# A clustered attention's slot in another order: scores between the two groups of transposes, the exponential between their evictions, the row maximum between the low parts

## The chip, the cores and the metric

One core of a Trainium2 chip. The time of a run is device microseconds from launch to end; the kernel before took 782.77 us in the median of three runs (782.29, 782.77 and 786.18).

## The reference

Attention over 2 batches, 8 heads, 768 positions of 64 elements: each query and key is assigned to the nearest of 16 centroids of its head, and a query attends only to keys of its own cluster. Two MLP layers follow on the 1536 rows of 512 elements.

```python
q_assign = argmax(q_n @ c_n.T); k_assign = argmax(k_n @ c_n.T)
scores = where(q_assign[..., :, None] == k_assign[..., None, :], (q @ k.T) / 8, -1e9)
attn = softmax(scores)                 # rows of 768
x = (attn @ v) laid out as [1536, 512]
x = softplus(x @ w_in1) @ w_out1       # 512 -> 2048 -> 512
h = x @ w_in2
out = (h * clip(h + 3, 0, 6) / 6) @ w_out2
```

## The kernel before

Everything is computed in pairs of a high and a low part: a value is rounded to fp32r (the high part), and the remainder is the low part; products of the parts are summed in PSUM.

The attention runs over 8 pairs of heads (2 batches x 4 pairs). A pair has 12 slots: 2 heads x 6 tiles of 128 query rows. So there are 96 slots. In each slot one tile of queries goes through these steps, named by the functions that issue them:

- `scores(t)`, line 403: four matmuls (512 and 256 columns, two terms each) into a score tile `s` of PSUM. There are two such tiles.
- `row_max(t)`, line 414: VectorE reduces the 768 columns to the negated maximum `nm`.
- `expo(t)`, line 419: ScalarE takes the exponential into the probability tile `pr`, with the row sums read from the accumulator.
- `flip(t, g)`, line 429, for g = 0 and 1: three transposes of `pr` into a PSUM tile `t` (two tiles in all, so a group uses the tile of the same group a slot earlier), then the eviction: ScalarE copies `t` to the high part `pth` (line 442), and VectorE subtracts to make the low part `ptl` (line 443). A tile `t` is free when its low part is done.
- `weigh(h, c)`, line 445: four matmuls of 384 columns of an earlier half head (three slots) with the values.
- `gather(h, step)`, line 458: after every third slot the finished half head is taken out of PSUM by two ScalarE copies of 64 partitions, one into `rest` and one into `main`; GpSimd adds them later. The product of head 0 of a pair has its main part on partitions 0 to 63 and head 1's on 64 to 127.

The order of the work is written by hand (`tc.manual_schedule`). Each engine takes its instructions strictly in the order of the code, and waits for semaphores where tiles demand it. The loop over slots (line 817) has seven places, 0 to 6, between its steps; `at(slot, place, function, ...)` puts the other work there: loading and splitting the next pair's q and k, its cluster masks (`p_sims` to `p_mask`, lines 293 to 368: similarities, their maximum, one-hot, transposed back), their assembly by DMA into the operands `Q` and `K` (`assemble`, `assemble_mask`), the sums' reciprocals (`total`, `tot_flip`), and weights of the first MLP layer. In the text o is the first of the 12 slots ahead of a pair in which its masks are made.

The MLPs follow: 96 steps of 24 matmuls of 512 columns, from some 256 us to the end.

## Time and profile before

| what | value |
|---|---|
| median of three runs | 782.77 us |
| profiled execution | 782.03 us, its span 780.2 us |
| TensorE busy | 768.9 us, 99% of the span |
| VectorE, ScalarE, GpSimd busy | 456.3, 416.9 and 151.0 us |
| granted TensorE clock | 0.999 |
| slots 0 to 95 | from 17.8 to some 250 us |

A busy time is the time in which an engine's records cover the clock. TensorE's matmuls overlap one another, so that a busy engine may still be held up; the weight loads (PEld) of a matmul stand in a row of their own, and waits of TensorE mostly show there. The waits and the timeline name the instruction that waited and, after the arrow, whose end released it.

### The profile page before, as it was taken

To read this page: it belongs to the slowest core of one execution; us is meant where nothing else is said; L and a number is where in the kernel's file an instruction comes from. 1 tells how busy PE (TensorE), PEld (TensorE's weight loads), DVE (VectorE), ACT (ScalarE), POOL (GpSimd) and SP (SyncE) were. 2 spreads that over 40 slices of the span, in tenths; PEclk is the share of its full clock that TensorE was granted. 3 is DMA by queue.
4 is the path that set the end of the run, shared out by engine and by line. 5 is a ranking of instruction groups with operands and counts; after the bars stand their busy time and mean duration, and the time that the engine had idled before them with its cause. 6 is when DMAs were issued, how large, how long until landed. Compare 5 with 4: busy or idle time off the path is not lost.

```text
span 780.2 us, 10575 instructions
## 1 busy us (share of the span) xinstructions
PE 768.9 (99%) x3841; PEld 642.1 (82%) x3841; DVE 456.3 (58%) x788; ACT 416.9 (53%) x830; POOL 151.0 (19%) x222
## 2 busy tenths in 40 slices
PE   7999999999999999999999999999999999999998
PEld 6788888888888788888888888888888888888886
DVE  6988888888988999721111276879752322232222
ACT  6899988988998766522122254545532222222221
POOL 3666756856434000000000000000000000000000
PEclk9999999999999999999999999999999999999999
DMA  7647667557381760000000365640000100010001
GB/s 190 186 128 178 145 158 188 136 157 172 87 249 56 267 240 0 1 1 0 1 1 27 110 207 176 210 135 0 1 1 0 55 1 0 1 55 0 1 1 54
DMA packets 39124, 69.75 MB, mean 89 GB/s; under 512 B 4480, under 2 KB 24096, under 8 KB 39072
## 3 DMA queue, kind: packets, MB, share of 16 engines
q1 hardware_dynamic: 39072, 69.08, 30.9%
q8 instruction: 30, 0.49, 0.3%
q14 instruction: 22, 0.18, 0.1%
HBM read 46.30 MB, written 3.19 MB: 63 GB/s over the span
## 4 chain that ended last, share of the span: by engine, by line
PE 88%; DVE 5%; ACT 3%; issue 1%; POOL 1%; DMA 1%; POOLq 0%; ACTq 0%; DVEq 0%; SPq 0%
PE h L169 32%; PE y L895 17%; PE y L893 16%; PE t L438 7%; PE s L408 6%; PE pv L453 6%; PE psm L308 2%; DVE ptl L443 1%; DVE nm L416 1%; ACT pth L442 1%; ACT pr L424 1%; DMA rsb<-row 0%; DMA row<-rT 0%; PE warm L245 0%; ACT xs L468 0%
## 5 line engine op out<-in xcount | busy, mean ns | idle before, releaser
L169 PE MATMUL h<-xhi,pi 128*128 128x512 f32 x768 | 238.5, 392 | 0.6 <-DVE pi L144 0.5
L169 PEld LDWEIGHTS h<-xhi,pi 128*128 128x128 f32 x768 | 143.8, 188 | 32.3 <-DVE pi L144 1.0
L874 DVE TENSOR_TENSOR glo<-g,ghi 128x512 fp32r<-128x512 f32 x96 | 66.3, 691 | 146.2 <-ACT ghi L861 117.4
L169 PE MATMUL h<-xlo,pi 128*128 128x512 f32 x384 | 149.9, 390 | 0.0
L895 PE MATMUL y<-po,ghi 128*128 128x512 f32 x384 | 118.9, 391 | 0.0
L893 PE MATMUL y<-ghi,po 128*128 128x512 f32 x384 | 118.8, 391 | 0.0
L443 DVE TENSOR_TENSOR ptl<-t,pth 128x384 fp32r<-128x384 f32 x192 | 97.8, 550 | 28.0 <-ACT pth L442 27.8
L867 DVE SCALAR_TENSOR_TENSOR g<-u,h 128x512 f32<-128x512 f32 x48 | 33.0, 688 | 127.2 <-ACT u L863 127.1
L863 ACT ACTIVATE u<-h,half 128x512 f32<-128x512 f32 x48 | 33.0, 687 | 128.3 <-PE h L169 128.0
L416 DVE TENSOR_REDUCE nm<-s 128x1 f32<-128x768 f32 x96 | 90.7, 945 | 3.7 <-PE s L408 3.7
L442 ACT ACTIVATE pth<-t 128x384 fp32r<-128x384 f32 x192 | 85.7, 487 | 11.8 <-PE t L438 11.4
L408 PE MATMUL s<-K,Q 128*128 128x256 f32 (+1 forms) x384 | 89.9, 356 | 1.7 <-ACT pr L424 1.1
L438 PE MATMUL t<-ident,pr 128*128 128x128 f32 x576 | 88.3, 280 | 1.2 <-DVE ptl L443 0.7
L424 ACT ACTIVATE pr<-s,nm 128x768 f32<-128x768 f32 x96 | 86.5, 901 | 3.5 <-DVE nm L416 3.2
L860 ACT ACTIVATE g<-h 128x512 f32<-128x512 f32 x48 | 28.5, 595 | 110.8 <-PE h L169 110.8
L169 PEld LDWEIGHTS h<-xlo,pi 128*128 128x128 f32 x384 | 72.1, 188 | 15.7
L895 PEld LDWEIGHTS y<-po,ghi 128*128 128x128 f32 x384 | 72.1, 188 | 15.6
L893 PEld LDWEIGHTS y<-ghi,po 128*128 128x128 f32 x384 | 72.0, 188 | 15.6
L438 PEld LDWEIGHTS t<-ident,pr 128*128 128x128 f32 x576 | 64.0, 140 | 20.4 <-DVE ptl L443 15.4
L408 PEld LDWEIGHTS s<-K,Q 128*128 128x128 f32 x384 | 65.8, 189 | 11.5 <-ACT pr L424 2.3
L895 PE MATMUL y<-po,glo 128*128 128x512 f32 x192 | 75.1, 391 | 0.0
L893 PE MATMUL y<-glo,po 128*128 128x512 f32 x192 | 75.0, 391 | 0.0
(123 smaller groups left out, 937.9 us busy)
## 6 DMA issues: line engine op xcount, KB each, us to landing
ri<-in_moe_w_in SPq DMA_DIRECT2D x29, 512.0 KB, 4.6
ro<-in_moe_w_out SPq DMA_DIRECT2D x29, 512.0 KB, 4.8
K<-hik SPq DMA_DIRECT2D x31, 192.0 KB, 5.3
Q<-hiq SPq DMA_DIRECT2D x15, 384.0 KB, 4.1
Q<-loq SPq DMA_DIRECT2D x16, 192.0 KB, 5.6
v<-in_v SPq DMA_DIRECT2D x8, 384.0 KB, 6.6
rsb<-row SPq DMA_DIRECT2D x16, 192.0 KB, 3.8
out<-o SPq DMA_DIRECT2D x12, 256.0 KB, 3.5
```

The costliest lines, as they stand in the source:

```text
L169: nc.tensor.matmul(hs[n][:, :TB], w[:, c, :], x[c][:, cols], start=(c == 0 and i == 0), stop=(c == NC - 1 and i == 2))
L408: nc.tensor.matmul(ps[:, n0:n1], Q[i][:, u, j * P:(j + 1) * P], K[i][:, u, n0:n1], start=(u == 0), stop=(u == 1),)
L416: nc.vector.tensor_reduce(nm, st_s[t][:, :S], AX.X, ALU.max, negate=True)
L424: nc.scalar.activation(pr, st_s.pop(t)[:, :S], AF.Exp, bias=st_p[t], accum_out=sums_of[n][:, i, j:j + 1])
L438: nc.tensor.transpose(pt[:, c * P:(c + 1) * P], pr[:, kt * P:(kt + 1) * P], ident)
L442: last_flip[:] = [nc.scalar.activation(dh, src, AF.Copy)]
L443: nc.vector.tensor_tensor(dl, src, f32(dh), ALU.subtract)
L453: nc.tensor.matmul(st_v[h][:, :HALF], vs[:, kt, i, :], st_t[h][u][:, kt, :], start=(kt == 0 and u == 0), stop=(kt == NJ - 1 and u == 1),)
L863: nc.scalar.activation(t["u"], t["h"], AF.Relu, bias=half, scale=1.0 / 6.0)
L874: nc.vector.tensor_tensor(t["glo"], t["g"], f32(t["ghi"]), ALU.subtract)
L893: nc.tensor.matmul(y[:, :TB], w[:, e, :], x, **fl)
L895: nc.tensor.matmul(y, x[:, e * P:(e + 1) * P], w.rearrange("p c e -> p (c e)"), **fl)
```

## The change

In a slot the transposes of group 0 now come first, then the scores of the slot three ahead, then the transposes of group 1, then the weighing. On ScalarE the copy of group 0 comes first, then the exponential of the slot two ahead (it was one ahead, so three `pr` buffers), then the copy of group 1. On VectorE the row maximum of the slot three ahead (it was two) stands between the two low parts.

TensorE in two slots of the second pair's time (`t` transposes, `s` scores, `pv` weighing), before:

```order
L438 MATMUL t<-ident,pr 128x128 x6
L408 MATMUL s<-K_155,Q_153 128x512 x2
L408 MATMUL s<-K_155,Q_153 128x256 x2
L453 MATMUL pv<-pth,vs 128x384
L453 MATMUL pv<-ptl,vs 128x384
L453 MATMUL pv<-pth,vs 128x384
L453 MATMUL pv<-ptl,vs 128x384
L483 MATMUL pb<-ident,rs 12x128
L438 MATMUL t<-ident,pr 128x128 x6
```

and now:

```order
L438 MATMUL t<-ident,pr 128x128 x3
L408 MATMUL s<-K_156,Q_154 128x512 x2
L408 MATMUL s<-K_156,Q_154 128x256 x2
L438 MATMUL t<-ident,pr 128x128 x3
L453 MATMUL pv<-pth,vs 128x384
L453 MATMUL pv<-ptl,vs 128x384
L453 MATMUL pv<-pth,vs 128x384
L453 MATMUL pv<-ptl,vs 128x384
L438 MATMUL t<-ident,pr 128x128 x3
L408 MATMUL s<-K_157,Q_155 128x512 x2
L408 MATMUL s<-K_157,Q_155 128x256 x2
L438 MATMUL t<-ident,pr 128x128 x3
```

The block of six transposes is cut into three and three, with the scores between them.

ScalarE in the slots after a head's gathering (`pth` copies, `pr` exponential, `xs` gathering, `sT` similarities), before:

```order
L424 ACTIVATE pr,sums<-s,nm 128x768
L466 ACTIVATE xs_1004<-pv 64x384
L468 ACTIVATE xs_1003<-pv 64x384
L442 ACTIVATE pth<-t 128x3x128 x2
L314 ACTIVATE sT<-psm,c_r 128x384
L424 ACTIVATE pr,sums<-s,nm 128x768
L442 ACTIVATE pth<-t 128x3x128 x2
L424 ACTIVATE pr,sums<-s,nm 128x768
```

and now:

```order
L442 ACTIVATE pth<-t 128x3x128
L468 ACTIVATE xs_1107<-pv 128x384
L442 ACTIVATE pth<-t 128x3x128
L424 ACTIVATE pr,sums<-s,nm 128x768
L442 ACTIVATE pth<-t 128x3x128 x2
L424 ACTIVATE pr,sums<-s,nm 128x768
L442 ACTIVATE pth<-t 128x3x128 x2
L424 ACTIVATE pr,sums<-s,nm 128x768
```

The copies no longer stand in pairs; a copy of group 1 is followed by the next slot's copy of group 0 (x2). The gathering shown is one of head 0: a single copy of 128 partitions where there were two of 64.

VectorE, numbers kept (`ptl` low parts, `nm` row maximum), before:

```order
L416 TENSOR_REDUCE nm_1105<-s_1093 128x1
L443 TENSOR_TENSOR ptl_1112<-t_1113,pth_1111 128x3x128
L443 TENSOR_TENSOR ptl_1112<-t_1119,pth_1111 128x3x128
L416 TENSOR_REDUCE nm_1144<-s_1126 128x1
L443 TENSOR_TENSOR ptl_1112<-t_1146,pth_1111 128x3x128
L443 TENSOR_TENSOR ptl_1112<-t_1152,pth_1111 128x3x128
```

and now:

```order
L443 TENSOR_TENSOR ptl_1008<-t_1096,pth_1007 128x3x128
L443 TENSOR_TENSOR ptl_1112<-t_1113,pth_1111 128x3x128
L416 TENSOR_REDUCE nm_1126<-s_1121 128x1
L443 TENSOR_TENSOR ptl_1112<-t_1128,pth_1111 128x3x128
L443 TENSOR_TENSOR ptl_1112<-t_1145,pth_1111 128x3x128
L416 TENSOR_REDUCE nm_1160<-s_1155 128x1
L443 TENSOR_TENSOR ptl_1112<-t_1162,pth_1111 128x3x128
```

Each maximum stands between the low parts of one slot.

Further: for head 0 of a pair `gather` copies all 128 partitions at once into `main`, and a DMA moves the other half into `rest` (16 copies less, 16 DMAs more). The steps of the mask making are put at other places of their slots, mostly after the slot's transposes. The tile `eq` is bf16 and the one-hot is made in place. The centroids lie in the tile of v, with the part that is needed longer copied by GpSimd to `cT`; the zeroing of `oh` goes from VectorE to GpSimd, and some small tiles share a buffer.

```diff
--- before
+++ after
@@ -176,7 +176,7 @@
             ld = st_ld.enter_context(tc.tile_pool(name="ld", bufs=1, side="right"))
             tp = st_ld.enter_context(tc.tile_pool(name="tp", bufs=2, side="right"))
             qk = pool("qk", 1)
-            pp = pool("pp", 2)
+            pp = pool("pp", 3)
             vsp = pool("vs", 2)
             ptp = pool("ptp", 2)
             xs_p = pool("xs", 1)
@@ -213,8 +213,8 @@
                 raws[n, "v"] = t
 
 
-            cent = cb.tile([P, NPAIR * (C + D)], F32, name="cent")
-            cT = cent[:, :NPAIR * C].rearrange("p (n c) -> p n c", c=C)
+            cent = ld.tile([P, S], F32, tag="v", name="cent")[:, :NPAIR * (C + D)]
+            cT = cb.tile([P, NPAIR, C], F32, name="cT")
             c_sb = cent[:, NPAIR * C:].rearrange("p (n d) -> p n d", d=D)
             load_qk(0, "q", lambda: nc.sync.dma_start(cent, centroids))
             load_qk(0, "k")
@@ -332,7 +332,7 @@
             def p_equal(n):
                 d = prep[n]
                 sv, mx = d["pb"], d["mx"]
-                eq = sm.tile(full, F32, tag="eq", name="eq", bufs=1)
+                eq = sm.tile(full, BF16, tag="eq", name="eq", bufs=1)
                 nc.vector.tensor_tensor(eq, sv, mx.unsqueeze(2).to_broadcast(full), ALU.is_equal)
                 d["eq"] = eq
 
@@ -349,8 +349,8 @@
 
             def p_first(n):
                 d = prep[n]
-                oh = sm.tile(full, BF16, tag="oh", name="oh", bufs=1)
-                nc.vector.tensor_tensor(oh, d["eq"], d["mx2"].unsqueeze(2).to_broadcast(full), ALU.is_equal)
+                oh = d["eq"]
+                nc.vector.tensor_tensor(oh, oh, d["mx2"].unsqueeze(2).to_broadcast(full), ALU.is_equal)
                 d["oh"] = oh
 
             def p_onehot(n):
@@ -462,7 +462,12 @@
                     xs_of[n, hf] = [xs_p.tile([P, HALF], F32, tag=f"xs{u}", name=f"xs{u}", bufs=(4, 2)[u]) for u in range(2)]
                 pv = st_v[h]
                 main, rest = xs_of[n, hf]
-                if step == 0:
+                if i == 0:
+
+                    if step == 0:
+                        nc.scalar.activation(main, pv[:, :HALF], AF.Copy)
+                        nc.sync.dma_start(rest[a:a + D], main[z:z + D])
+                elif step == 0:
                     nc.scalar.activation(rest[a:a + D], pv[z:z + D, :HALF], AF.Copy)
                 elif step == 1:
                     nc.scalar.activation(main[a:a + D], pv[a:a + D, :HALF], AF.Copy)
@@ -484,7 +489,7 @@
                 sums_of[n] = pb
 
             def tot_out(n):
-                rT = sm.tile([2 * NJ, P], F32, tag="rT", name="rT", bufs=1)
+                rT = sm.tile([2 * NJ, P], F32, tag="sT", name="rT", bufs=1)
                 nc.scalar.activation(rT, sums_of[n][:2 * NJ, :P], AF.Copy)
                 row = dr.tile([2, S], F32, tag="row", name="row")
                 nc.sync.dma_start(row.rearrange("h (j t) -> (h j) t", t=P), rT)
@@ -548,14 +553,14 @@
                     at(o + 0, 4, p_sims_out, n)
                     at(o + 1, 1, p_back, n)
                     at(o + 1, 4, p_max, n)
-                    at(o + 2, 2, p_equal, n)
+                    at(o + 2, 4, p_equal, n)
                     at(o + 2, 4, p_rank, n)
-                    at(o + 4, 2, p_best, n)
-                    at(o + 5, 2, p_first, n)
-                    at(o + 6, 3, p_onehot, n)
-                    at(o + 7, 1, p_mask, n)
+                    at(o + 4, 4, p_best, n)
+                    at(o + 5, 4, p_first, n)
+                    at(o + 6, 4, p_onehot, n)
+                    at(o + 6, 6, p_mask, n)
                     at(o + 4, 1, assemble, n, 0)
-                    at(o + 7, 2, assemble_mask, n, 0)
+                    at(o + 7, 1, assemble_mask, n, 0)
                     at(o + 10, 5, assemble, n, 1)
                     at(o + 11, 4, assemble_mask, n, 1)
                     at(o + -3, 6, load_v, n)
@@ -584,8 +589,8 @@
                 o += 2 * SL
                 if n < NP - 1:
                     at(o + -2, 4, total, n)
-                    at(o + 3, 0, tot_flip, n)
-                    at(o + 3, 4, tot_out, n)
+                    at(o + 3, 4, tot_flip, n)
+                    at(o + 3, 6, tot_out, n)
                     at(o + 4, 4, tot_spread, n)
                     for hf in range(2):
                         if n < NP - 2:
@@ -693,7 +698,7 @@
             at(99, 3, lambda: convert_rest(*pieces0[5], engine=nc.vector))
 
 
-            c_sq = sm.tile([P, HALF], F32, tag="eq", name="c_sq", bufs=1)[:, :NPAIR * D].rearrange("p (n d) -> p n d", d=D)
+            c_sq = sm.tile([P, HALF], F32, tag="mk", name="c_sq", bufs=1)[:, :NPAIR * D].rearrange("p (n d) -> p n d", d=D)
             c_ss = cb.tile([P, NPAIR], F32, name="c_ss")
             c_n = cb.tile([P, NPAIR], F32, name="c_n")
             c_r = cb.tile([P, NPAIR], F32, name="c_r")
@@ -719,6 +724,7 @@
                     nc.tensor.transpose(warm[:, :P], ident, ident)
 
 
+            nc.gpsimd.tensor_copy(cT.rearrange("p n c -> p (n c)"), cent[:, :NPAIR * C])
             p_centroids(0)
             clear(1)
             p_split_hi(0, "q", 0)
@@ -750,8 +756,8 @@
             p_back(0)
             warm_up(14)
 
-            oh = sm.tile(full, BF16, tag="oh", name="oh", bufs=1)
-            nc.vector.memset(oh, 0.0)
+            oh = sm.tile(full, BF16, tag="sT", name="oh", bufs=1)
+            nc.gpsimd.memset(oh, 0.0)
             prep[0]["oh"] = oh
 
             def one_head(i, parts=range(5)):
@@ -816,26 +822,25 @@
             p_values(0, 1)
             for s in range(-3, NS + 7):
                 extras(s, 0)
-                if 2 <= s + 1 < NS:
-                    expo(s + 1)
+                if 0 <= s < NS:
+                    flip(s, 0)
                 extras(s, 1)
                 if 2 <= s + 2 < NS:
-                    row_max(s + 2)
+                    expo(s + 2)
                 extras(s, 2)
-                if 0 <= s < NS:
-                    flip(s, 0)
+                if 2 <= s + 3 < NS:
+                    scores(s + 3)
+                    row_max(s + 3)
                 extras(s, 3)
                 if 0 <= s < NS:
                     flip(s, 1)
                 extras(s, 4)
-                if 2 <= s + 3 < NS:
-                    scores(s + 3)
                 extras(s, 5)
                 h, c = s // JH - 1, s % JH
                 if 0 <= h < 4 * NP:
                     weigh(h, c)
                     if c == JH - 1:
-                        for step, where in enumerate((2, 2, 4)):
+                        for step, where in enumerate((0, 0, 4)):
                             at(s + 1, where, gather, h, step)
                 extras(s, 6)
             assert not extra, extra
```

## Rows read from the trace of the kernel before

**Rows 1.** The page's first part: busy us, share of the span, instructions of each engine
```profile
PE 768.9 (99%) x3841; PEld 642.1 (82%) x3841; DVE 456.3 (58%) x788; ACT 416.9 (53%) x830; POOL 151.0 (19%) x222
```

**Rows 2.** Windows: stretch, sum of length, busy us (instructions) by engine, clock, DMA
```profile
140.00:160.00 20.00, 19.99 (x129) 16.85 (x129) 17.93 (x31) 19.02 (x45) 17.16 (x24) 1.00 0.60 145
320.00:340.00 20.00, 20.00 (x90) 16.56 (x89) 6.95 (x12) 5.45 (x10) 0.00 (x0) 1.00 0.00 0
```

**Rows 3.** Waits from 34 to 230 us: who waited for whom, total us, times, longest
```profile
PEld t L438 <- DVE ptl L443: 13.1, 61, 0.5
...
PEld s L408 <- ACT pr L424: 0.9, 3, 0.5
```

**Rows 4.** Timeline of TensorE in a slot without waits: start, us, engine, line, count
```profile
231.66 0.82 PE L438 MATMUL t<-ident,pr 128*128 128x128 f32 x6
232.24 0.94 PE L408 MATMUL s<-K,Q 128*128 128x512 f32 x4
233.02 0.33 PE L453 MATMUL pv<-pth,vs 128*128 128x384 f32 x1
...
233.72 0.82 PE L438 MATMUL t<-ident,pr 128*128 128x128 f32 x6
```

**Rows 5.** Timeline of weight loads for transposes (PEld), two slots with waits
```profile
145.82 0.31 PEld L438 LDWEIGHTS t<-ident,pr 128*128 128x128 f32 x3 [0.17 <-DVE ptl L443]
146.29 0.31 PEld L438 LDWEIGHTS t<-ident,pr 128*128 128x128 f32 x3 [0.15 <-DVE ptl L443]
...
148.07 0.31 PEld L438 LDWEIGHTS t<-ident,pr 128*128 128x128 f32 x3
```

**Rows 6.** Timeline of ScalarE (ACT) in the same stretch
```profile
143.68 0.48 ACT L466 ACTIVATE xs<-pv 64x384 f32<-64x384 f32 x1
144.18 0.49 ACT L468 ACTIVATE xs<-pv 64x384 f32<-64x384 f32 x1
...
145.60 0.88 ACT L424 ACTIVATE pr<-s,nm 128x768 f32<-128x768 f32 x1
...
146.48 0.89 ACT L442 ACTIVATE pth<-t 128x384 fp32r<-128x384 f32 x2
147.26 0.90 ACT L424 ACTIVATE pr<-s,nm 128x768 f32<-128x768 f32 x1
```

**Rows 7.** Timeline of VectorE (DVE) in the same stretch
```profile
145.21 1.02 DVE L443 TENSOR_TENSOR ptl<-t,pth 128x384 fp32r<-128x384 f32 x2 [0.38 <-ACT pth L442]
146.15 0.95 DVE L416 TENSOR_REDUCE nm<-s 128x1 f32<-128x768 f32 x1
147.02 0.54 DVE L348 TENSOR_REDUCE mx<-eq 128x24 f32<-128x384 f32 x1
147.47 1.01 DVE L443 TENSOR_TENSOR ptl<-t,pth 128x384 fp32r<-128x384 f32 x2
```

**Rows 8.** Timeline: a slot's six transposes on TensorE
```profile
139.17 0.82 PE L438 MATMUL t<-ident,pr 128*128 128x128 f32 x6
```

**Rows 9.** Timeline of ScalarE: the eviction of rows 8
```profile
139.69 0.87 ACT L442 ACTIVATE pth<-t 128x384 fp32r<-128x384 f32 x2 [0.51 <-PE t L438]
```

**Rows 10.** Timeline of all engines in the first slots
```profile
12.31 0.36 DVE L775 TENSOR_TENSOR oh<-eq,mx 128x192 bf16<-128x192 f32 x1
...
18.37 1.98 POOL L282 TENSOR_TENSOR lok<-k,hik 128x384 fp32r<-128x384 f32 x2 [7.96 <-ACT hik L268]
19.47 1.10 DVE L775 TENSOR_TENSOR oh<-eq,mx 128x192 bf16<-128x192 f32 x1
...
21.00 0.67 ACT L367 ACTIVATE mk<-po,mbi,msc 128x384 fp32r<-128x384 bf16 x1 [0.36 <-PE po L361]
...
23.61 0.58 SPq L397 DMA_DIRECT2D Q<-mk  x1
...
26.19 0.94 PE L408 MATMUL s<-K,Q 128*128 128x512 f32 x4
```

**Rows 11.** The mask's transfers (line 397) over the whole run
```profile
DMA to landing us min/median/max: 1.8/2.0/5.0
```

## The prediction, made before the changed kernel ran

> **What bounds the kernel now.** I read the busy times first. TensorE is busy for 99% of the span [rows 1], so one might stop there. But its records overlap, and the windows say little more: 19.99 of 20 us in a stretch of the attention, 20.00 in one of the MLPs [rows 2]. In the attention ScalarE (19.02 of 20) and VectorE (17.93) are nearly full too [rows 2]; three engines hand each slot round in a ring, and each is held to its written order.
>
> So the waits come next. From 34 to 230 us, some seven pairs of heads (28 us each), the weight loads of the transposes waited 61 times and 13.1 us for a low part, that is, for VectorE to free a tile `t`; those of the scores waited 0.9 us for an exponential [rows 3]. These 14.0 us, 2.0 per pair, are what a better order can win there. The timeline confirms that they are lost time: a slot without waits takes 233.72 - 231.66 = 2.06 us (transposes 0.58, scores 0.78, weighing 0.70) [rows 4]; one with waits of 0.17 and 0.15 takes 148.07 - 145.82 = 2.25 [rows 5].
>
> The weight loads are busy for 16.85 us of 20 in the attention and 16.56 in the MLP stretch [rows 2]; in the latter matmul follows matmul without a wait, so a load share of 16.6 is a full TensorE. The Trainium skill (Perfetto Trace Analysis, Identifying the Most-Contended Engine) says that matmul busy time is no good measure of TensorE's headroom, and names the busy share of the weight loads instead. The first half the trace bears out; by the second the attention would have 16% to give, 31 us of these 196, and the time would be 752. By the waits it is 14. I take the waits.
>
> **The change part by part: the slot.** Durations: transposes to the start of their copy 139.69 - 139.17 = 0.52 [rows 8, 9]; a copy of 384 columns 0.49 [rows 6], and the next activation starts 0.39 after it (two copies, 147.26 - 146.48 = 0.78) [rows 6]; exponential with its sums 146.48 - 145.60 = 0.88 until the next starts [rows 6]; a low part 0.55 (two in 1.02, so the second starts 0.47 after the first), a row maximum 0.87 until the next starts [rows 7].
>
> The new slot, from the start of its first transposes at 0: scores at 0.29, transposes of group 1 at 1.07, weighing at 1.36, next slot at 2.06. ScalarE: copy 0 from 0.52, exponential from 0.91, copy 1 from 1.79 to 2.28, free at 2.18 for what can overlap; the next copy 0 can start at 2.58, so 0.40 is to spare. VectorE: low part 0 at 1.05, maximum at 1.52, low part 1 from 2.39 to 2.94, free at 2.86; next low part 0 at 3.11, so 0.25 is to spare. Group 1 of the next slot wants its tile `t` at 2.06 + 1.07 = 3.13: a slack of 0.19. A plain slot therefore runs without a wait.
>
> Gatherings and mask steps disturb it. The two copies of a gathering start 0.50 apart and end the ScalarE spare: 0.48 + 0.49 [rows 6], about 1.0 before copy 0. Now head 0 needs one such copy, 0.5: 0.40 is spare, so everything moves by 0.10, within the slack. Head 1 still needs 1.0: 0.60 late, 0.41 beyond the slack, and TensorE waits that long. Of head 1's two gatherings per pair one falls in slot o, whose six similarity matmuls of 384 columns (weighing's four take 0.70 [rows 4], so six take 1.05) give ScalarE more time than it needs. On VectorE each of the four mask steps of 0.45 (147.47 - 147.02) [rows 7] exceeds the spare by 0.20; they come in two neighbouring pairs of slots, and the second of each makes group 1 wait 0.2. Together 0.41 + 2 x 0.2 = 0.8 us per pair stay.
>
> The same reckoning for the old order: low part 1 ends at 2.05 and group 1 of the next slot wants its tile at 2.35; any gathering of 1.0 after the exponential costs 0.46, four times a pair, and the mask steps add 0.4: 2.2 against 2.0 measured (less for slot o). So it can be trusted to some 0.3 per pair. Gain: 14.0 - 7 x 0.8 = 8.4 us. Its ends: 14.0 when nothing stays, and 0 when all stays.
>
> **The other parts.** The 16 new DMAs stand in SP's queue at place 0 of a slot, waiting for a ScalarE copy that is issued just before; behind them come the mask's transfers, a slot (2.06 us) later. That slot hides them: 0; without it, the 0.58 of one issue [rows 10] on two slots of seven pairs, at most 8 us.
>
> The start. The first pair's second mask (`mk`, at 21.00) now stands behind the exponential of slot 3 (0.88), which waits for a maximum (0.87) that now follows the one-hot step on VectorE: 1.75 later. Its last transfer was issued at 23.61, transfers land 2.0 after issue [rows 11], so at 25.6, and the scores that need it started at 26.19 [rows 10]: 0.6 in hand. Cost 1.75 - 0.6 = 1.1 us; from 0 (if the steps before it speed up as well) to 2.6 (if nothing is in hand and a maximum more stands in front).
>
> GpSimd's copy of the centroids stands ahead of the first similarity matmuls. No row shows one of 64 columns; one of 384 takes 0.99 [rows 10]. Between 0 and 0.99; in proportion to the columns it is 0.16, and I take 0.2. The end: the last exponential comes a slot earlier, so the last slots, which have no scores, may shorten: 0 to 1, I take 0.3. The bf16 `eq` and the in-place one-hot: not shown; the one-hot step took 0.36 alone and 1.10 while GpSimd ran a subtraction [rows 10], so seven of them differ by -2 to +5 us in all if every one met or missed GpSimd; they stand behind low parts with 0.25 to spare, and I take 0. The zeroing on GpSimd has until that step's input is ready: 0. Waits of the MLPs do not change, since their stage starts earlier as a whole.
>
> Sum: 8.4 - 1.1 - 0.2 + 0.3 = 7.4 us off the profiled execution's 782.0, 774.6. The median of the runs stands 0.7 above that execution, so the forecast is 775.4 us.
>
> **The rivals.** (1) All waits go: 14.0 instead of 8.4, 769.8. For it: spare time on all engines, and ScalarE has 16 copies of 0.49 less. Against it: head 1's gathering is as long as before.
>
> (2) The wait only changes its place, and the time stays: 782. Group 1's copy now stands behind an exponential, and the slack is 0.19 in each slot. If the chain is 0.29 longer than I reckon, every plain slot waits 0.10, and 84 of them give back the 8.4. For it: a ring of three full engines [rows 2]. The copies no longer come in pairs; an exponential right behind a copy still starts 0.11 before that ends (147.26 against 146.48 + 0.89) [rows 6], so no overlap need be lost. The Trainium skill (ScalarE: Activation LUTs, What ACT_TABLE_LOAD costs) says that activations back to back overlap by about 93 ns, which these rows bear out. What the rule holds against the change is that a copy that has to wait for its transposes is not back to back: two of them lose an estimated 0.19 per slot by the page's figure, the whole slack. By it the time lies between the forecast and this rival; by the rows it is the forecast.
>
> (3) Slower: the copy behind the exponential makes every slot late. Low part 1 now ends a slot's chain: transposes, copy 0, exponential, copy 1, low part 1. From the point where it ends more than 0.19 late in a plain slot TensorE pays each further tenth in every one of 84 slots. With 0.36 late it is 84 x 0.17 = 14.3, and with the 5.6 that stay and the 1.0 at start and end 20.9 against the 14.0 of now: 789.7. For it: the copy of group 1 moved from 0.39 to 1.27 behind copy 0. Against it: VectorE's own order would hold low part 1 until 2.39 anyhow, 0.11 after copy 1 ends, so only a delay of both counts.
>
> **How the numbers follow.** The forecast (771.5 to 779) 0.54; rival 1 (below 771.5) 0.12; rival 2 (779 to 786) 0.21; rival 3 (above 786) 0.13. About 0.5%, 3.9 us, is what a measurement of this kernel can tell from no change: faster is below 778.9, slower above 786.7. Faster: 0.54 + 0.12, and a little less for the border, 0.65; same 0.22; slower 0.13. The range for 8 in 10 goes from 769, which leaves out some 0.05 of rival 1, to 785, which leaves out rival 3. The forecast's own range is 771.5 to 779.
>
> **What the changed kernel's profile would show.** The step on the slot is right if TensorE's waits for low parts fall from 13.1 us to about 5, those left being mostly of the second group and in slots with head 1's gathering, and if plain slots take 2.06. It is wrong if waits for a low part stand in nearly every slot (rival 2 or 3), or if none are left (rival 1). The gathering is right if 16 ScalarE copies of 128 partitions stand where 32 of 64 did. The start is right if the first scores of head 1 begin about 27.3. A wait of the scores for a mask transfer in later pairs, or of a copy for the exponential ahead of it with TensorE idle, would make the forecast wrong.

## The result and the profile after

The changed kernel takes 787.49 us in the median of ten runs, the kernel before 782.25 in ten beside them: a ratio of 1.0061, 95% interval 1.0048 to 1.0075. It is slower by 5.2 us, where 775.4 was forecast and 769 to 785 was the range. The profiled executions are 787.78 and 782.03 us long.

Where the 5.8 us of the two spans arose is read from four marks in the timelines: the first transposes of slots 0, 12 and 84, and the load of the activation table behind the attention's last eviction (lines 860 and 865). The table lists the experiments too; times in us, "first" is the first pair, slots 0 to 11, "end" goes from slot 84 to the table load, and "MLPs after" from there to the end of the span. A row's parts are of one profiled execution, its median is of all runs; e3's profiled execution (784.70) was the slowest of its twelve runs.

| kernel | first | slots 12 to 83 | end | MLPs after | median |
|---|---|---|---|---|---|
| before | 31.85 | 171.92 | 29.12 | 529.6 | 782.25 |
| changed | 32.40 | 172.97 | 33.26 | 529.6 | 787.49 |
| e3: old order, all other parts | 36.60 | 168.97 | 30.02 | 529.7 | 783.36 |
| e4: old order, merged gathering alone | 33.56 | 168.23 | 29.90 | 530.0 | 780.12 |
| e13: new order, two copies | 31.89 | 175.48 | 33.59 | 529.6 | 791.44 |
| e14: old order, repaired | 30.09 | 170.04 | 28.99 | 530.9 | 779.50 |

So 4.1 of the 5.8 us lie in the last twelve slots, 1.1 in the six middle pairs, which were to give 7 us, and 0.5 in the first pair.

The page's first part, for the changed kernel (before: [rows 1]), shows TensorE at 97% instead of 99%, and ScalarE 8 us shorter, as 16 copies of 128 partitions should make it:

```profile
PE 765.7 (97%) x3841; PEld 644.9 (82%) x3841; DVE 460.9 (59%) x787; ACT 408.7 (52%) x814; POOL 150.7 (19%) x224
```

In the stretch of the attention TensorE is busy for 19.45 of 20 us, where it was 19.99 [rows 2]:

```profile
140.00:160.00 20.00, 19.45 (x130) 17.41 (x129) 18.53 (x30) 17.77 (x43) 15.54 (x23) 1.00 0.53 130
```

The waits of the weight loads from 34 to 230 us (before: [rows 3]):

```profile
PEld t L438 <- DVE ptl L443: 7.1, 19, 1.3
PEld L361 <- DVE eq L353: 3.0, 5, 0.7
PEld s L408 <- DMA K<-mk: 1.6, 3, 0.8
PEld s L408 <- DMA Q<-mk: 1.2, 1, 1.2
PEld s L408 <- issue: 0.5, 2, 0.4
PEld pbk L321 <- ACT sT L314: 0.5, 3, 0.2
...
```

Waits for low parts are 19 where there were 61. In their place stand waits for the one-hot tile `eq` and for the mask's transfers, which the kernel before did not have here. The plain slot is what was reckoned, 145.23 - 143.16 = 2.07 us on TensorE's timeline (before, 2.06: [rows 4]); the scores stand between the groups:

```profile
143.16 0.49 PE L438 MATMUL t<-ident,pr 128*128 128x128 f32 x3
143.41 0.95 PE L408 MATMUL s<-K,Q 128*128 128x512 f32 x4
144.20 0.49 PE L438 MATMUL t<-ident,pr 128*128 128x128 f32 x3
144.44 0.42 PE L453 MATMUL pv<-pth,vs 128*128 128x384 f32 x1
...
145.23 0.49 PE L438 MATMUL t<-ident,pr 128*128 128x128 f32 x3
```

A slot with an extra step is longer: of pair 1 to 5's 29.1 us, 1.7 are lost (27.4 = 12 slots of 2.06, twelve similarity matmuls of 0.175, and 0.57 for the small transposes). The largest loss is the one-hot step; all engines around it in the changed kernel:

```profile
148.04 1.03 POOL L476 TENSOR_TENSOR xs<-xs,xs 128x384 f32<-128x384 f32 x1
...
148.35 1.01 DVE L443 TENSOR_TENSOR ptl<-t,pth 128x384 fp32r<-128x384 f32 x2
...
152.62 1.01 POOL L378 TENSOR_TENSOR vs<-v,vs 128x384 fp32r<-128x384 f32 x1
...
152.90 1.15 DVE L353 TENSOR_TENSOR eq<-eq,mx 128x384 bf16<-128x384 bf16 x1
...
154.10 0.17 PEld L361 LDWEIGHTS <-eq 128*128 128x128 bf16 x3 [0.71 <-DVE eq L353]
```

The same step in the kernel before, timeline of VectorE and GpSimd:

```profile
149.27 0.55 DVE L353 TENSOR_TENSOR oh<-eq,mx 128x384 bf16<-128x384 f32 x1
...
149.31 1.38 POOL L378 TENSOR_TENSOR vs<-v,vs 128x384 fp32r<-128x384 f32 x1
```

Whichever of the two starts first keeps its time, and the other gets longer: before, VectorE was 0.04 us ahead and GpSimd paid; now GpSimd is 0.28 ahead and VectorE, and TensorE behind it, pay. Low parts, which read one input from PSUM and one from SBUF, are not stretched: two at 148.35 take 1.01 us, as elsewhere [rows 7], though the first starts inside a two-input step of GpSimd. 60 others of the changed kernel start so, and all 61 take 0.54 to 0.56 us.

The second loss is in slot 9, where the scores wait for the mask's transfers. In pair 5, SP's queue, the mask and the scores' load:

```profile
183.41 0.67 ACT L367 ACTIVATE mk<-po,mbi,msc 128x384 fp32r<-128x384 bf16 x1
183.61 1.18 SPq L502 DMA_DIRECT2D rsb<-row  x2
...
184.83 0.60 SPq L469 DMA_DIRECT2D xs<-xs  x1
185.53 0.56 SPq L397 DMA_DIRECT2D Q<-mk  x1
...
188.31 0.19 PEld L408 LDWEIGHTS s<-K,Q 128*128 128x128 f32 x1
...
188.81 0.53 PEld L408 LDWEIGHTS s<-K,Q 128*128 128x128 f32 x3 [0.32 <-DMA K<-mk]
```

and in the kernel before:

```profile
180.62 1.17 SPq L497 DMA_DIRECT2D rsb<-row  x2
...
181.97 0.67 ACT L367 ACTIVATE mk<-po,mbi,msc 128x384 fp32r<-128x384 bf16 x1
...
182.67 0.56 SPq L397 DMA_DIRECT2D Q<-mk  x1
...
186.46 0.77 PEld L408 LDWEIGHTS s<-K,Q 128*128 128x128 f32 x4
```

From the mask to the scores there is more time than before (4.90 us to their first load, 4.49 before). But the first transfer used to be issued when the mask was done, and now it is issued 1.45 us after that, behind the reciprocals' transfers (`rsb`) and the gathering's new one (`xs`).

At the end, in the changed kernel, VectorE's, ScalarE's and the weight loads' timelines between slot 92 and the table load:

```profile
247.75 0.72 DVE L117 TENSOR_SCALAR val<-val 128x512 uint32<-128x512 uint32 x1
248.50 1.38 DVE L119 SCALAR_TENSOR_TENSOR val<-ri,val 128x512 uint32<-128x512 uint32 x1
249.81 1.01 DVE L443 TENSOR_TENSOR ptl<-t,pth 128x384 fp32r<-128x384 f32 x2
...
250.41 0.31 PEld L438 LDWEIGHTS t<-ident,pr 128*128 128x128 f32 x3 [1.60 <-DVE ptl L443]
...
252.76 0.63 ACT L133 ACTIVATE pi<-val 128x512 fp32r<-128x512 f32 x1 [1.28 <-DVE val L123]
...
254.80 0.19 PEld L169 LDWEIGHTS h<-xhi,pi 128*128 128x128 f32 x1 [1.16 <-POOL pi L144]
...
256.40 1.28 ACT L865 ACT_TABLE_LOAD   x1
```

The steps that convert the MLP's weights (lines 109 to 144, one piece of the weights at a time) stand in slots by number. In the new slots they fall between two low parts (0.72 and 1.38 us, beside GpSimd; 0.42 and 0.69 without it, under e14) and in front of an eviction (line 133, 252.76); and one matmul group of the third MLP block (254.80) now stands ahead of the last transposes and waits for its weights.

### The profile page after: what moved, and what is told of

Read it like the earlier page. It is cut to its first block, busy times and chain, and to the rows that moved or that the text cites. A ratio compares the mean times of both kernels' runs of the same rounds, so it can differ in the third digit from the quotient of the medians.

```text
span 786.0 us, 10639 instructions
## 1 busy us (share of the span) xinstructions
PE 765.7 (97%) x3841; PEld 644.9 (82%) x3841; DVE 460.9 (59%) x787; ACT 408.7 (52%) x814; POOL 150.7 (19%) x224
## 4 chain that ended last, share of the span: by engine, by line
PE 82%; DVE 7%; ACT 5%; issue 2%; POOL 2%; DMA 1%; SPq 1%; POOLq 0%; ACTq 0%; DVEq 0%
PE h L169 33%; PE y L900 17%; PE y L898 16%; PE pv L453 5%; PE t L438 5%; PE s L408 4%; DVE nm L416 2%; PE psm L308 2%; DVE ptl L443 2%; ACT pr L424 2%; ACT pth L442 1%; DMA K<-mk 1%; DVE eq L353 1%; ACT xs L473 1%; SPq L397 0%
## 5 line engine op out<-in xcount | busy, mean ns | idle before, releaser
L443 DVE TENSOR_TENSOR ptl<-t,pth 128x384 fp32r<-128x384 f32 x192 | 104.6, 550 | 28.1 <-ACT pth L442 27.9
L442 ACT ACTIVATE pth<-t 128x384 fp32r<-128x384 f32 x192 | 94.4, 492 | 24.2 <-PE t L438 23.0
L438 PE MATMUL t<-ident,pr 128*128 128x128 f32 x576 | 95.5, 275 | 4.3 <-DVE ptl L443 3.2
L408 PE MATMUL s<-K,Q 128*128 128x256 f32 (+1 forms) x384 | 91.7, 358 | 3.8 <-DMA K<-mk 2.1
L438 PEld LDWEIGHTS t<-ident,pr 128*128 128x128 f32 x576 | 69.2, 140 | 14.2 <-DVE ptl L443 10.3
```

Source lines behind the costliest of these rows:

```text
L408: nc.tensor.matmul(ps[:, n0:n1], Q[i][:, u, j * P:(j + 1) * P], K[i][:, u, n0:n1], start=(u == 0), stop=(u == 1),)
L438: nc.tensor.transpose(pt[:, c * P:(c + 1) * P], pr[:, kt * P:(kt + 1) * P], ident)
L442: last_flip[:] = [nc.scalar.activation(dh, src, AF.Copy)]
L443: nc.vector.tensor_tensor(dl, src, f32(dh), ALU.subtract)
```

## The experiments

"Old order" is the order before the change. Unless told otherwise an edit is made to the changed kernel, and runs stand beside runs of the kernel before (782.2 to 782.3).

### e3, e4 and e13: the order, the merged gathering, and both

e3 takes back the loop and the places of mask steps, gatherings and reciprocal transposes. e4 is the kernel before with

```diff
-                if step == 0:
+                if i == 0:
+                    if step == 0:
+                        nc.scalar.activation(main, pv[:, :HALF], AF.Copy)
+                        nc.sync.dma_start(rest[a:a + D], main[z:z + D])
+                elif step == 0:
```

and e13 is the changed kernel without these lines. (`i` is 0 for head 0.)

> All parts of the change but the order: slots, mask steps, gatherings and reciprocal transposes stand where they stood before the change; the merged gathering, the bf16 tiles, the third probability buffer and the centroid copy stay. Theory A (the order gains in plain slots and loses as much in disturbed ones, the rest is harmless): the merged gathering takes 0.5 us of ScalarE from two gatherings of four per pair, worth 0.2 to 0.46 each, so 776 to 780 us, below both kernels. Rival B (the parts beside the order cost the time, the bf16 one-hot or the 16 new transfers): 784 to 787.5 us, above the kernel before.

> The kernel before with the merged gathering alone (for head 0 one ScalarE copy of 128 partitions and a transfer, in place of two copies of 64). Theory A: 14 gatherings shorter by 0.5 us on ScalarE are worth 0.2 to 0.46 each in the old order, 776 to 779.5 us. Rival B (the second copy was hidden, or the transfer on the queue delays the mask or the assembly): 781.5 to 783 us. Against the kernel with all parts but the order it shows what bf16 and the other parts cost.

> The changed kernel with two ScalarE copies per gathering, as before the change, in place of one and a transfer for head 0; the new order stays. In the old order the merged gathering took 0.66 us off a pair (28.87 to 28.21) and made slots 7 to 11 plain (2.05). Theory A (the order has 0.4 us spare on ScalarE, so a pair of copies costs 0.4 to 0.6 more there): pairs 1 to 5 take 29.7 to 30.2 us, 790 to 794 us, so the order alone costs 8 us or more and the merged gathering hid half of it. Rival B (the new order makes plain slots by itself, the gathering is worth nothing in it): 29.0 to 29.3 per pair, 786.5 to 788.

Measured: 783.36 (ratio 1.0002, 0.9988 to 1.0017), 780.12 (0.9975, 0.9962 to 0.9988), and 791.44 (1.0114, 1.0098 to 1.0130). With the merged gathering alone a pair takes 28.2 us instead of 28.9, and slots 7 to 10 are plain in the old order as well (2.05); the weight loads' waits in e4 from 50 to 224 us are

```profile
PEld t L438 <- DVE ptl L443: 7.8, 37, 0.5
...
```

With the new order and two copies (e13) a pair takes 29.5. So the merging helps in either order (0.6 and 0.4 per pair, by the table's third column), and the order costs: by the medians 4.1 us between e3 and the changed kernel, by the profiled executions 4.0 in slots 12 to 83 and 3.2 at the end, less the 4.2 that e3's first pair lost. e13 and the kernel before, both with two copies, differ by 3.6 and 4.5 in these two parts, and by 9.3 in the medians.

e13's theory A had the time right (790 to 794) and the pair a little too long (29.7 to 30.2). e4 and e3 fell between their theories, e4 0.6 above its theory A. In e3 it was the first pair (36.60): TensorE stood from 40.93 to 43.01 us for the second pair's mask and from 45.83 to 47.60 for an exponential, and from about 44 to 51 us its granted clock was 0.50, the lower of its two levels (1.2 GHz); stretch, busy times, clock, DMA:

```profile
45.00:50.00 5.00, 3.23 (x11) 2.63 (x11) 3.26 (x7) 3.30 (x7) 4.06 (x5) 0.50 0.00 0
```

The mean clock of e3's runs goes from 1.000 (779.61 us, the fastest) to 0.995 (784.70), so its median holds some of this, and the parts outside the first pair tell the order's cost better.

### e2 and e5: type or neighbour of the one-hot step

e2, from the third pair on:

```diff
-                eq = sm.tile(full, BF16, tag="eq", name="eq", bufs=1)
+                eq = sm.tile(full, F32 if n > 1 else BF16, tag="mk" if n > 1 else "eq", name="eq", bufs=1)
-                oh = d["eq"]
+                oh = sm.tile(full, BF16, tag="eq", name="oh", bufs=1) if n > 1 else d["eq"]
```

> The changed kernel, with the mask's equality tile in float32 and the one-hot in a tile of its own, as before the change (from the third pair on, in tiles that are free then); places unchanged. Theory A (the bf16 one-hot step is what stretches beside GpSimd's subtraction): L353 takes about 0.55 us instead of 1.15, TensorE's 0.5 us wait for it in slot 6 of a pair goes, the masks come 0.6 earlier, and the scores' waits for mask transfers shrink: 5 pairs by 0.5 to 1.0, so 782.5 to 785 us. Rival B (it is the place, beside the subtraction, not the type): L353 still takes about 1.1 us and the time stays within 0.7 of 787.5.

Measured: 789.47; the step takes 1.00 us in the mean of the six float32 ones (0.96 for the same six in the changed kernel; 0.60 at the old place, in e3 with bf16 and in e4 with float32). That is rival B on the step, and the type is not the cause. The time is 2.0 above 787.5, outside rival B's band: the profiled execution's first pair takes 35.20 us, with a wait of 3.6 us for a mask's transfer and a granted clock of 0.50 from 45 to 48 us. e5 moves the neighbours, GpSimd's steps on a finished pair:

```diff
-                            at(o + 12 + 2 * hf, 5, fin_hi, n, hf)
-                            at(o + 16 + hf, 2 + hf, fin_lo, n, hf)
+                            at(o + 11, 4 * hf, fin_hi, n, hf)
+                            at(o + 11, 4 * hf + 1, fin_lo, n, hf)
```

> The changed kernel, with GpSimd's four steps on a finished pair (two copies, two subtractions, 3.0 us per pair) moved from the slots of the next pair's mask steps to slots 11 of the pair before, where GpSimd is idle for some 4 us. Nothing else moves; GpSimd's subtraction of the values then ends before the one-hot step, and a scaling with one input stands beside it. The type of the one-hot tile made no difference (float32 1.00 us, bf16 0.96 in the mean, against 0.60 at the old place with either type). Theory A (VectorE's step with two SBUF inputs waits when a two-input step of GpSimd has started before it): L353 falls to about 0.55 us, TensorE's 0.7 us wait for it in slot 6 goes, pairs 1 to 5 take 28.4 to 28.6 us instead of 29.1, and the time falls by 2.5 to 4 us to 783.5 to 785. Rival B (any GpSimd work beside it stretches it): L353 stays at 0.9 to 1.1 us and the time within 0.7 of 787.5.

Measured: 788.73. The step falls to 0.69 us and the wait for it from 3.0 to 1.4 us, but the scores now wait longer for what comes next; waits from 50 to 224 us in e5:

```profile
PEld t L438 <- DVE ptl L443: 3.2, 11, 0.3
PEld s L408 <- issue: 2.2, 3, 1.2
PEld s L408 <- DMA K<-mk: 2.0, 3, 0.9
PEld L361 <- DVE eq L353: 1.4, 5, 0.3
...
```

Both theories missed the time. The neighbour does stretch the step, as theory A has it (not quite all: a scaling of GpSimd's still stands beside it), but there is no gain: slot 6 got 0.3 us shorter and slot 9 0.4 longer. The mask was written no earlier than in the changed kernel (16.9 us after the start of pair 5 in both), and its transfers were issued no earlier (19.0 and 19.1), behind the same two others. So an earlier one-hot step only moves TensorE's wait to the end of SP's queue.

### e10: the chain a slot earlier

e5 with

```diff
-                    at(o + 4, 4, p_best, n)
-                    at(o + 5, 4, p_first, n)
-                    at(o + 6, 4, p_onehot, n)
-                    at(o + 6, 6, p_mask, n)
+                    at(o + 3, 4, p_best, n)
+                    at(o + 4, 1, p_first, n)
+                    at(o + 5, 4, p_onehot, n)
+                    at(o + 5, 6, p_mask, n)
...
-                    at(o + 7, 1, assemble_mask, n, 0)
+                    at(o + 6, 1, assemble_mask, n, 0)
```

> The changed kernel with GpSimd's four steps early (as in the run where the one-hot step fell from 0.96 to 0.69 us, the wait for it from 0.7 to 0.3, and the scores of slot 9 then waited for the mask's transfers, pair time unchanged at 29.1), and with the mask's last five steps one slot (2.06 us) earlier. Theory A (one chain, one-hot, transposes, mask, transfers, scores, is too late in the new order, because the scores that need it stand before the second group and the mask after the weighing): the scores' waits for masks and issues in pairs 1 to 5 (2.0 and 2.2 us in all) go, and a pair takes 28.3 to 28.6 instead of 29.1: 783.5 to 785 us. Rival B (steps put into neighbouring slots cost as much in waits for low parts): 28.9 to 29.2 per pair, 786.5 to 788.

Measured: 790.18, 29.4 per pair: rival B in kind, and above its band. The waits for masks go (one of 0.6 is left), and slot 5 takes 3.2 us instead of 2.06. VectorE, ScalarE and weight loads there:

```profile
151.80 0.78 DVE L353 TENSOR_TENSOR eq<-eq,mx 128x384 bf16<-128x384 bf16 x1
152.50 0.94 DVE L416 TENSOR_REDUCE nm<-s 128x1 f32<-128x768 f32 x1
...
153.53 0.90 ACT L424 ACTIVATE pr<-s,nm 128x768 f32<-128x768 f32 x1 [0.41 <-DVE nm L416]
...
153.96 0.31 PEld L438 LDWEIGHTS t<-ident,pr 128*128 128x128 f32 x3 [0.86 <-DVE ptl L443]
```

A late maximum makes the exponential late, the second copy stands behind that, and the low part and the next transposes behind the copy. In the old order both copies stand together, behind an exponential whose maximum was issued a slot ahead.

### e15 and e16: the exponential back behind the second copy

This is e15; e16 has the edits of e5 and e11 too.

```diff
-                if 2 <= s + 2 < NS:
-                    expo(s + 2)
                 extras(s, 2)
...
                     flip(s, 1)
+                if 2 <= s + 2 < NS:
+                    expo(s + 2)
```

> The changed kernel with one line moved: the exponential stands behind the second group's copy again (both copies, then the exponential), while the scores stay between the groups and the maximum between the low parts. Reckoned as before: copy 1 from 1.59 to 2.08, exponential to 2.86, copy 0 of the next slot 0.28 late, but low part 1 done at 2.55 and its tile wanted at 3.13, so 0.58 us of slack instead of 0.19. Theory A (the exponential in front makes the second copy hostage to every late maximum): waits for low parts in slots 3 and 4 and for the one-hot get shorter, pairs 1 to 5 take 28.2 to 28.7, 782 to 785 us. Rival B (the late first copy takes it back): 29 or more per pair, 787 or more.

> The kernel with the exponential behind the second copy, and with the repairs of GpSimd's steps and of the last slots. Theory A: 3 us less at the end and 0.3 per pair less than without the repairs, 778 to 781 us. Rival B: no better than without them, since the wait moves to the mask's transfers: 783 or more.

Measured: 827.01 and 826.71; both theories missed. Waits of e15 from 50 to 224 us:

```profile
PEld s L408 <- ACT pr L424: 30.8, 50, 0.7
```

I had left out the score tiles: there are two, and scores that stand between the groups need the one that the exponential of the slot before frees. So with two score tiles the exponential has to stand between the copies once the scores do; the moves come as a set.

### e6, e7 and e9: SP's queue in the first pair

In the changed kernel the second pair's first mask is written at 33.24 us, and its transfers are issued from 38.14 on, behind fetches of weights and the new transfer of the gathering:

```profile
33.24 0.67 ACT L367 ACTIVATE mk<-po,mbi,msc 128x384 fp32r<-128x384 bf16 x1
...
36.62 0.91 SPq L102 DMA_DIRECT2D ro<-in_moe_w_out  x2
37.63 0.47 SPq L469 DMA_DIRECT2D xs<-xs  x1
38.14 0.59 SPq L397 DMA_DIRECT2D Q<-mk  x1
```

e6 moves four fetches behind the mask's transfers, and their piece's conversion from slots 10 to 14 to 19 to 23; e7 does so in e4, and e9 fetches them in slots 68 to 74 and converts in 77 to 81.

```diff
-... ("o", ((4, 0), (4, 3), (5, 0), (5, 3), (7, 2), (7, 6)))):
+... ("o", ((8, 0), (8, 3), (9, 0), (9, 3), (10, 0), (10, 3)))):
```

> The changed kernel, with four fetches of the first output weights (128 KB each) moved from slots 4 and 5, in front of the second pair's mask transfers in SP's queue, to slots 8 and 9 behind them, and that piece's conversion from slots 10 to 14 to slots 19 to 23. In the profile of the changed kernel SP issues that mask's transfers 4.9 us after the mask is written, and the first scores of the second pair wait for them (1.2 us; 2.2 to 3.6 in three other kernels with the merged gathering, none before the change). Theory A (a queue in order, and busy transfer engines): the wait goes, slots 9 and 10 of the first pair take 2.1 to 2.5 us instead of 3.2 each, 1.2 to 2 us in all, 785.5 to 786.5. Rival B (the mask is late by itself, because its steps are): the wait stays at 1 us or more and the time within 0.7 of 787.5.

> The kernel before with the merged gathering (780.1 us) and the same four fetches behind the mask's transfers. Theory A: the 2.3 us that this kernel lost in slots 9 and 10 of its first pair (33.56 against 31.85 us for that pair) come back: 777.5 to 778.5 us, below every kernel so far. Rival B (the wait of 2.8 us for an exponential there has another cause): 779.5 to 780.5.

> The kernel before with the merged gathering (780.1 us) and the first output weights fetched with the later weights, in the pair that begins with slot 60, and converted in slots 77 to 81. Moving those fetches by only four slots took the wait out of the first pair (33.56 to 30.05 us) and put 1.7 us into the second (28.21 to 29.92), with no gain in the median. Theory A (the transfer engines are full in the first 45 us, so that any byte moved out of them counts): first pair about 30, second 28.2, 777.0 to 778.5 us. Rival B (the wait moves again, or the conversion costs as much at its new place): 779.5 to 780.5.

Measured: 789.49 (e6), 780.39 (e7) and 780.06 (e9; 0.9970, 0.9958 to 0.9982). The waits do go from the first pair (29.77, 30.05 and 30.34 us), as theory A has it, and come back: slot 15 takes 5.13 us in e6, the second pair 1.7 more in e7, and in e9 slot 77 takes 3.77, where VectorE's conversion meets the one-hot step and GpSimd. For the time it is rival B in e7 and e9; e6 is slower than both its theories.

### e1, e8, e11 and e12: the end

All four issue the third block's matmuls behind the last transposes, and move the conversion:

```diff
-            at(92, 4, convert_bits, *piece, 0)
-            at(93, 0, convert_bits, *piece, 1)
-            at(94, 2, convert_bits, *piece, 2)
-            at(94, 3, convert_parts, *piece, False)
-            at(94, 3, convert_rest, *piece)
+            at(93, 1, convert_bits, *piece, 0)
+            at(93, 4, convert_bits, *piece, 1)
+            at(94, 1, convert_bits, *piece, 2)
+            at(95, 2, convert_parts, *piece, False)
+            at(95, 3, convert_rest, *piece)
```

The sixth piece's steps go behind slot 95 as well. This is e11. In e1 the second step is at (93, 1) too and `convert_parts`, the split on ScalarE, at (94, 2); e8 has the split at (94, 2), and e5's and e6's edits; e12 is e11 with e9's and e10's.

> The changed kernel, with its last twelve attention slots put in order: the matmuls of the third MLP block are issued behind the attention's last transposes (as they stood before the change), and the conversion steps of the last two pieces of weights go to places where VectorE has no row maximum (slots 93 to 96). The result was 787.5 us against 782.3, and the stretch from slot 84 to the table load grew by 4.2 us. Theory A (these steps were tuned to the old order and now stand between low parts): most of the 4.2 comes back, 783.3 to 784.5 us, the stretch from slot 84 to the load of the activation table goes from 33.3 us to at most 30.5, and the wait of 1.2 us for the weights' low part is gone. Rival B (the last slots are longer because of the new order itself, whatever stands between): the stretch stays at 32 to 33 us and the time at 786.5 to 787.5.

> The changed kernel with all the repairs: GpSimd's steps early, the fetches behind the mask's transfers, the third MLP block's matmuls behind the last transposes, and the last weight steps spread singly over the gaps between low parts. Theory A (the new order is as good as the old one once nothing collides): 3 us from the one-hot, 1.5 from the queue, 2 to 3 from the last slots, 780 to 781.5 us, two to three us above the old order with the merged gathering and the moved fetches, because start and last slots stay longer. Rival B (the order itself loses time in every slot with an extra step): 783 to 786.

> The changed kernel with the last slots repaired again: third MLP block behind the last transposes, the three bit steps of the fifth weight piece singly between low parts, and its ScalarE split behind the first copy of slot 95 (in the run with all repairs that split stood ahead of a copy and waited 1.76 us for VectorE). Theory A (most of the 4.2 us that the end of the attention lost is such steps in front of copies and low parts): slot 84 to the table load takes 30.0 to 31.0 us instead of 33.3, and the time is 784.5 to 785.5. Rival B (new order): 32 us or more, 786.5 to 787.5.

> The changed kernel with the four repairs of this set together (late output weights, GpSimd's steps early, mask a slot earlier, last slots). Theory A (the order itself costs nothing once nothing collides): 0.6 us per pair, 1.5 in the first pairs, 2.5 at the end, 780 to 782 us, the time of the kernel before, but still 2 to 4 above the old order with merged gathering and late weights. Rival B (the order loses in every slot with an extra step): 784 or more.

Measured: 787.69 (e1), 788.26 (e8), 786.44 (e11; 1.0048, 1.0034 to 1.0062), 788.85 (e12). The end takes 32.09, 31.88, 30.16 and 29.75 us instead of 33.26. e1 is rival B (the time 0.2 above its band); e8 is slower than both its theories; e11 has theory A's end and close to rival B's time. The steps do lengthen the end, once the split stands behind the first copy of slot 95. In e8 ScalarE's split still stood ahead of two copies:

```profile
254.57 0.63 ACT L133 ACTIVATE pi<-val 128x512 fp32r<-128x512 f32 x1 [1.76 <-DVE val L123]
255.10 0.85 ACT L443 ACTIVATE pth<-t 128x384 fp32r<-128x384 f32 x2
```

Of e11's 3.1 us, 1.6 come back behind the table load (531.2 instead of 529.6): that work was moved past the mark and not saved. The median moves by 1.0, with intervals that overlap. With all repairs (e12) the time is rival B's, and slots 12 to 83 take 179.3 us, 6.3 more than in the changed kernel. Of these, 3.2 are in the second pair, where TensorE stood from 55.24 to 57.04 us and its granted clock was then 0.50 from 58 to 61, and 1.6 in pair 6, where the conversion now stands. The other pairs lose 0.2 to 0.6 each, about as in e10. So e12 does not show that the order itself makes every extra step dear.

### e14: a version below both kernels

e9 with the conversion in slots 78 to 81, and GpSimd's steps on the last but one pair behind the last transposes:

```diff
-                            at(o + 7 + hf, 2, fin_scale, n, hf)
+                            at(o + 12, hf, fin_scale, n, hf)
...
```

> The old order with merged gathering and late output weights (780.1 us), with that piece's conversion in slots 78 to 81 (it stood beside the one-hot step of slot 77 and made that slot 3.77 us) and GpSimd's six steps on the last but one pair behind the attention's last transposes (VectorE's weight steps took 0.75 and 1.38 us beside them instead of 0.42 and 0.69, and the transposes behind waited 1.77). Theory A (collisions of VectorE and GpSimd on two-input steps): pair 6 takes 28.0 or less instead of 29.2, slot 84 to the table load 29.0 instead of 30.0, 777.5 to 778.8 us. Rival B (the waits come back elsewhere, or GpSimd's steps now slow the first MLP blocks): 779.5 to 781.

Measured: 779.50 (0.9964, 0.9951 to 0.9978), the lowest median, within rival B's band; pair 6 takes 28.3 us instead of 29.2 and the end 28.99 instead of 30.05, close to theory A, and the MLPs give back 1.3. VectorE's conversion in e9 beside GpSimd:

```profile
241.12 0.75 DVE L117 TENSOR_SCALAR val<-val 128x512 uint32<-128x512 uint32 x1
241.55 1.19 POOL L508 TENSOR_TENSOR xs<-xs,rsb 128x384 f32<-128x384 f32 x1
241.91 1.38 DVE L119 SCALAR_TENSOR_TENSOR val<-ri,val 128x512 uint32<-128x512 uint32 x1
```

and in e14 without it:

```profile
239.41 0.42 DVE L117 TENSOR_SCALAR val<-val 128x512 uint32<-128x512 uint32 x1
239.86 0.69 DVE L119 SCALAR_TENSOR_TENSOR val<-ri,val 128x512 uint32<-128x512 uint32 x1
```

## Why the prediction was wrong

**Right:** the plain slot, 2.07 against 2.06; the gathering's 16 copies; two of the waits for low parts that stay (0.29 and 0.28 us at 147.63 and 148.96, against 0.41 and 0.2); and at the start the mask 1.67 us later (22.67 us, where it was 21.00 [rows 10]; 1.75 was reckoned). Its scores wait 0.64 us, until 26.64, where a cost of 1.1 and 27.3 were forecast. GpSimd's copy of the centroids cost nothing: the first transposes of slot 0 start at 17.77 us, before at 17.80 (its price came from a subtraction's row). Signs that were to prove the forecast wrong were named, and one came: scores waiting for a mask's transfer in later pairs.

**The step that failed first** is "Together 0.41 + 2 x 0.2 = 0.8 us per pair stay". Measured are 1.7. Missing were the stretched one-hot step (0.6 per pair by its waits, of which the sum had 0.2; its stretching was put at 0, with "0.25 to spare" as its cover), the scores' wait for the mask's transfers (0.3) and 0.2 in slot 1, where the transposes of `sT` wait for ScalarE. For the scores' wait, I priced the new DMA in SP's queue as hidden, because the mask's transfers come a slot (2.06 us) later; in the trace they come 0.70 us behind it, and the reciprocals' transfers, moved by the change too, stand there as well. For the one-hot step the profile had the row: 0.36 alone and 1.10 beside a subtraction [rows 10], which I spread over chance instead of asking what stands beside the new place. The Trainium skill (SBUF — State Buffer, SBUF: two separate sides) says that VectorE, with two SBUF inputs or in a two-port mode, and GpSimd share a pair of ports as an exclusive lock, and that whichever starts first holds it for the whole instruction. The rows above agree (0.55 and 1.38, then 1.01 and 1.15), and so do the low parts, which have one SBUF input and are not stretched.

**The second** is the 14.0 us taken as what can be won, 2.0 per pair. The kernel before lost 1.5 per pair (28.9 less 27.4): a weight load's wait partly passes while earlier matmuls still stream, so the listed waits are more than the time. The prediction's own slot had shown it, with 0.32 us of waits listed and 0.19 lost. That its reckoning of the old order (2.2) agreed with the 2.0 was therefore luck. Of the 1.4 us by which a pair missed its forecast, 0.9 are the first step and 0.5 this one. And e4 shows that 0.6 of it is the merged gathering's, in the old order. The order's own share, between e3 and the changed kernel, is a loss.

**The third** is "The end ... may shorten: 0 to 1, I take 0.3": it grew by 4.1. I looked at the slots without scores and not at the weight steps written into them by number, which the diff does not touch and which get other neighbours. By e11 these steps and the one misplaced matmul group make 3.1 of it by the mark, and 1.5 once what comes back in the MLPs is taken off. What the rest is stays open; that it is the order's is argued, not shown.

**Smaller:** "the 16 new DMAs ... 0". In the middle pairs one stands right in front of the mask's transfers (0.60 us at 184.83, ahead of a wait of 0.32). Whether it or the later `rsb` causes the wait was not tested by itself; without it e13, whose mask comes 0.4 us later, still waits 0.26 there. In the first pair one stands in front of a mask's transfers in a queue that is 4.9 us behind, where the kernel before was 3.8 behind without it, and TensorE waits 1.2 us (3.6 in e2). Some of what varies there is the granted clock, which fell to 0.50 in e2 and e3; why the wait itself varies from kernel to kernel was not settled.

No rival was this. Rival 3 had the size (789.7) by late plain slots, and those are on time.

## What to carry to other kernels

When a slot's order is changed, every step that sits in it by number moves too: list each of them with its new neighbours on its engine, on GpSimd if it reads only SBUF, and in the DMA queue, up to the last slot. A listed wait of a weight load is not yet lost time: compare the slot's length with that of a slot without waits. A slot that just fits has no room for extra steps, and what a step costs there is read from a slot that has one. A change of several parts is priced part by part: here one part alone gained, and the order that it came with lost more.

## What was not expected of the hardware

- The lock between VectorE and GpSimd can go by some hundredths of a microsecond: 0.04 us ahead, VectorE takes 0.55 us and GpSimd 1.38; 0.28 behind, VectorE takes 1.15. Float32 or bf16 makes no difference (1.00 and 0.96 in the mean).
- It also holds for VectorE's integer steps on SBUF: 0.75 and 1.38 us beside GpSimd, 0.42 and 0.69 without. VectorE's low parts, with one input in PSUM, are free of it (61 of 61).
- When fetches were moved out of the start, a wait left the first pair and one of about its size came up in the second: 2.6 us out, 3.0 in (e6). In e12, where the same fetches come far later, it stands there too.
- After TensorE had stood for 1.3 to 3.3 us its granted clock was 0.50 for some 3 us in the profiled executions of e2, e8 and e12 and for some 7 in that of e3; in e4 it stood for 2.5 us and the clock stayed at 1.00.
